# A gated mix of an S4 and an H3 long convolution: the instruction order of three engines listed in the source, and the first gated group's transform moved ahead of the tables

## The chip, the cores and the metric

The kernel runs on one core of a Trainium2 chip, as one launch. The metric is the device time of that core in microseconds. It is given as the median of several executions, beside one execution that the hardware profiler recorded.

## What is computed

A sequence x of 2048 steps and 448 channels in bfloat16 goes through two long causal convolutions, one kernel per channel, and a gate mixes the two:

```python
x = A_u                                                   # [1, 2048, 448]
g = sigmoid((x * gate_w).sum(-1, keepdims=True))
# a: S4. The kernel K is made from 256 complex modes per channel.
logdA = exp(log_dt) * (A_re + 1j * A_im);  dB = exp(log_dt) * (B_re + 1j * B_im)
K = einsum("dn,dnl,dn->dl", C, exp(logdA * l), dB).real   # [448, 2048]
a = causal_conv(x, K) + x * Dskip
# b: H3. A shift convolution of four taps, then a long one with given kernels.
kv = sum(k_shifted_by_t * shift_k[:, t] for t in range(4)) * v
b = x * (causal_conv(kv, ssm_k) + kv * ssm_D)
out = g * a + (1 - g) * b
```

causal_conv is done by FFTs of twice the length in the reference.

## The kernel before

**Groups.** The 448 channels are split into four groups H of 28 channels on each of four partition quarters. Each group goes through the H3 path ("B", H) and the S4 path ("A", H), eight steps in the order B0, B1, B2, A0, B3, A1, A2, A3 (`seq`, L825). Names in code type are tiles as the profile shows them, or functions.

**A convolution as matmuls.** A sequence of one group is `spread` by PE matmuls (L215, PSUM tile `ps_c`), evacuated by ACT to a tile `zs` (`zsK` for an S4 kernel), and `transform`ed in place (L227, matmuls with the constant `s2_W` into `ps`, evacuated by ACT over `zs`). A copy with the two partition halves exchanged, `zsS`, is made by a DMA (L603, function `swapped`). The spectra of two sequences are multiplied on DVE (`products`, L286: first zsS, then zs, times the other's zs). `stage_a` (L265, `ps_a`, evacuated by ACT to `U`) and `stage_b` (L279, `ps_b`, with the constant `sb_G`) go back to the time domain. What ends a group, its epilogue, multiplies ps_b by `uu` into `ug` on DVE (L733, H3) or has ACT copy ps_b to a held tile (S4). The last S4 group is weighted by the gate and added to ug, which is then stored (L743 to L738).

**The S4 kernels.** They are made in eight blocks of 14 channels per quarter, two to a group. First come tables of exponentials: `Tables` builds `ks_hold` (scaled modes, L434), and `chunk(h)` makes one group's table `ET` for two blocks. DVE writes phases to `ks_ph` (L489), ACT takes Sin of them (L493) and Exp of the magnitudes (L481, `ks_mag` and the rows of ET), DVE multiplies (L506). Chunk 0 reads ks_hold in SBUF. `save` (L467) writes ks_hold to DRAM as `xfd`, and later chunks read it back as `ks_xf` (L476). Sin, Exp and Tanh each need an activation table on ACT, and a change between them is a table load. Then `KGen.block(j)` runs: a chain of DVE products and sums (L318 into `kg_P`, L323 into `kg_TQ` and `kg_TP`, L328, L332, L343), 224 matmuls of 21 rows into the one PSUM tile `pk` (L371), an ACT evacuation to `kg_S`, a gather by matmuls (L412, `ps_g` to `kg_KT`), and a spread with the constant WcK (`ps_c` to zsK).

**The front.** SP issues the input DMAs in program order: kt (the H3 k with its halo), the modes, `skraw(0)`, vt, uu, and then, where the source asks for them, `skraw(H)` of the later groups (`load_sk`, L587). `sk_cols` lets GpSimd (POOL) add ssm_D to the first column of skraw (L592), and the spread of KB[H] reads skraw after it. The shift convolution is a DVE product `kvt` (L651), PE sums into `ps_v` (L655) and ACT evacuations to kt; then `kv` = vt times kt (L680, four instructions). XB[H] is the spread and transform of kv. The gate multiplies uu by `gw` into ug (L812, seven instructions), sums by 14 matmuls into `ps_gate` (L815), reduces to `gt` (L817), and takes Tanh; gb and og are its copies. ug has the buffer of vt. `stage_b` of the constants makes `sb_G`: DVE phases `sb_ph`, ACT Sin `sb_v`, DVE multiplies `sb_G`.

**Buffers.** Eight buffers of tag q serve zs, zsS, zsK, kv, U, kvt, modes and the phases. One buffer of tag hq serves skraw, so that skraw(1) is loaded after skraw(0) is read. PSUM has three two-bank tiles of tag ps for everything else, and one for pk and ps_g.

**What sets the order.** The kernel is written as one long program; the framework's scheduler places each engine's instructions by a simulated timeline, with `high_priority` sections ahead of others. Some orders are fixed by hand. `after` ties an instruction behind another on one engine: the DVE chain of a block (`put`), block 0 behind kv, a chunk's phases behind the middle of the block (`kg.mid`), Exp and Sin by turns, s2_W's Sin behind the copy of the taps, and the final `mix` (L769) behind the last block's chain. `behind_other` holds the zsS DMAs of a step (through SP) until `kg_S` of its block is evacuated.

In the source the order around the change is: KB[0]'s spread, transform and swap; kv; chunk 0 and `save`; small constants; skraw(1)'s load and add; XB[0]'s spread, transform and products; the gate; then seven calls of `step(c, n, j)`. A step spreads the next group n, does stage_a of the current group c, transforms n, does stage_b of c, runs block j, and multiplies n's spectra. After them come block 7 and the last S4 group, in halves.

Of the kernel before, what the change touches and what calls it, by code (L numbers as in the profile page):

```python
# [17 lines left out]
P = 128  # L18
# [21 lines left out]


# [15 lines left out]

def low16(ap):
    return ap.bitcast(i16).rearrange("p (n t) -> p n t", t=2)[:, :, 0]


class Consts:

    def __init__(self, tc, pool, scratch):
        self.tc, self.nc, self.pool = tc, tc.nc, pool
        nc = self.nc
        self.scratch, self.used = scratch, 0
        self.pidx = pool.tile([P, 1], i32, name="c_pidx")
        nc.gpsimd.iota(self.pidx[:], pattern=[[0, 1]], base=0, channel_multiplier=1)
# [44 lines left out]
    def stage_2(self, b_col, off_col, big, behind):  # L114
        nc = self.nc
        W = self.pool.tile([P, 32, 2, 64], bf16, name="s2_W")
        j = self.iota("s2_j", [[32, 16], [1024, 64]], base=8)
        for k0 in (0, 16):
            if k0:
                for r in range(2):  # L120
                    nc.vector.scalar_tensor_tensor(out=off_col[r][:], in0=b_col[:], scalar=32.0 * k0, in1=off_col[r][:], op0=ALU.mult, op1=ALU.add)
            ph = big.tile([P, 16, 2, 64], i32, name="s2_ph", tag="kg_TQ", bufs=2)
            for r in range(2):
                self.phases(ph[:, :, r, :], j.rearrange("p (k s) -> p k s", k=16), b_col, off_col[r][:, 0:1])
            sn = nc.scalar.activation(W[:, k0:k0 + 16].rearrange("p k r s -> p k (r s)"),
                                 low16(ph[:].rearrange("p k r s -> p (k r s)")).rearrange("p (k c) -> p k c", k=16), ACT.Sin, scale=PHASE)
            after(self.tc, sn, behind)
        return W
# [11 lines left out]
    def stage_b(self, pool, qt, hqt, k_col, mask):  # L140
        nc = self.nc
        G = pool.tile([P, 64, 2, 4, 32], bf16, name="sb_G")
        jv = self.iota("sb_j", [[8, 16], [512, 32]]).rearrange("p (b a) -> p b a", b=16)
        offs = self.pool.tile([P, 4, 2], f32, name="sb_offs")
        for b0 in range(0, 64, 16):
            ph = qt([P, 16, 2, 32], "sb_ph", i32)
            for r, turn in enumerate((QUARTER, HALF)):
                o = offs[:, b0 // 16, r:r + 1]
                nc.vector.tensor_scalar(out=o, in0=k_col[:], scalar1=8.0 * b0, scalar2=turn, op0=ALU.mult, op1=ALU.add)
                self.phases(ph[:, :, r, :], jv, k_col, o)  # L150
            v = pool.tile([P, 16, 2, 32], bf16, name="sb_v", tag="kg_P4", bufs=2)
            nc.scalar.activation(v[:].rearrange("p b r a -> p (b r a)"), low16(ph[:].rearrange("p b r a -> p (b r a)")),
                                 ACT.Sin, scale=PHASE)
            for g in range(4):
                nc.vector.tensor_scalar(out=G[:, b0:b0 + 16, :, g, :], in0=v[:], scalar1=mask[:, g:g + 1], scalar2=None, op0=ALU.mult)
        return G

# [132 lines left out]
class KGen:  # L290

    def __init__(self, tc, pool, pk, psk, cons, sel_d, d4, ET):
        self.tc, self.nc, self.pk, self.psk = tc, tc.nc, pk, psk
        self.pool, self.cons, self.sel_d, self.d4, self.ET = pool, cons, sel_d, d4, ET

    def block(self, j, evac, behind=None):
# [5 lines left out]

        chain = [behind]

        def put(op):
            if chain[0] is not None:
                after(self.tc, op, chain[0])
            chain[0] = op

        def mult(srcs, e):  # L310
            P4 = self.pool.tile([P, 4, 2, 2, M], bf16, name="kg_P4", tag="kg_P4", bufs=2)
            r = EQ[:, entry_of(e) + 1] if e in Q_LEVELS else EP[:, entry_of(e) - EQ_N + 1]
            i = 0
            for src in srcs:
                m = src.shape[1]
                in0 = src.rearrange("p n c m -> p n (c m)").unsqueeze(2).to_broadcast([P, m, 2, 2 * M])
                in1 = bass.AP(r.tensor, r.offset, [list(r.ap[0]), [0, m], [-M, 2], [1, 2 * M]])
                put(V.tensor_tensor(out=P4[:, i:i + m].rearrange("p n v c m -> p n v (c m)"), in0=in0, in1=in1, op=ALU.mult))  # L318
                i += m
            return P4[:, 0:i].rearrange("p n v c m -> p (n v) c m")  # L320

        def add(T, dst, v):
            put(V.tensor_tensor(out=T[:, dst:dst + v.shape[1] // 2].rearrange("p n v m -> p (n v) m"), in0=v[:, :, 0], in1=v[:, :, 1], op=ALU.add))  # L323

        def back(i0, i1):
            lo = TP[:, 0:16]
            src = bass.AP(lo.tensor, lo.offset + (15 - i0) * 2 * M, [list(lo.ap[0]), [-2 * M, i1 - i0], [M, 2], [1, M]])
            put(V.tensor_tensor(out=TP[:, 16 + i0:16 + i1], in0=src,  # L328
                                in1=EP[:, E_R - EQ_N + i0:E_R - EQ_N + i1].unsqueeze(2).to_broadcast([P, i1 - i0, 2, M]), op=ALU.mult))

        q4 = mult([EQ[:, 0:2].unsqueeze(1)], 4)
        put(V.tensor_copy(TQ[:, 0], EQ[:, 0:2]))  # L332
# [6 lines left out]
        self.mid = chain[0]  # L339
# [3 lines left out]
        put(V.tensor_copy(TP[:, 0], EP[:, 0:2]))  # L343
# [17 lines left out]
        self.last = chain[0]  # L361
# [56 lines left out]
class Tables:  # L418

    def __init__(self, tc, pool, qt, hqt, psum, raw, ident, dt, xfd, dma):  # L420
        nc, V = tc.nc, tc.nc.vector
        self.tc, self.nc, self.pool, self.psum, self.raw, self.ident, self.qt, self.hqt = tc, nc, pool, psum, raw, ident, qt, hqt
        self.xfd, self.dma = xfd, dma
        self.exp, self.sin = None, None
# [44 lines left out]
    def chunk(self, h, behind=None):  # L469
# [7 lines left out]
        x, f = xf[:, :, 0], xf[:, :, 1]  # L477
        turn = 65536.0 / (2.0 * math.pi)

        def exps(dst, e):  # L480
            ex = nc.scalar.activation(dst, x, ACT.Exp, scale=float(e))  # L481
            if self.sin is not None:
                after(self.tc, ex, self.sin)
            self.exp = ex

        def unit(dst, e, off, first):
            ph = self.pool.tile([P, nb, 2, M], i32, name="ks_ph", tag="ks_ph", bufs=2)
            for c in range(2):
                op = V.tensor_scalar(out=ph[:, :, c], in0=f, scalar1=e * turn, scalar2=off + (QUARTER if c == first else 0.0),  # L489
                                     op0=ALU.mult, op1=ALU.add)  # L490
                if behind is not None:
                    after(self.tc, op, behind)
            sn = nc.scalar.activation(dst.rearrange("p b c m -> p b (c m)"),  # L493
                                      low16(ph[:].rearrange("p b c m -> p (b c m)")).rearrange("p (b x) -> p b x", b=nb), ACT.Sin, scale=PHASE)
            after(self.tc, sn, self.exp)
            self.sin = sn
# [24 lines left out]
        for i in range(NR):  # L521
            exps(ET[:, :, E_R + i], 8 * (2 * i + 1))
# [3 lines left out]
def body(  # L526
# [20 lines left out]
    nc = tc.nc  # L547
# [36 lines left out]
    def load_sk(H):  # L584
        raw = hqt([P, NC, 64], "skraw")
# [26 lines left out]
    cons = Consts(tc, wp, kgp.tile([P, 3584], i32, name="scratch", tag="kg_TP"))  # L612
# [17 lines left out]
    for g in range(4):  # L630
        nc.sync.dma_start(vt[g * 32:(g + 1) * 32], v4[g])  # L631
    uu = natt([P, 64, 112], "uu", "natu")
# [13 lines left out]
    wtc = nc.scalar.copy(wt, wraw.rearrange("p l t -> p t l")[:, ::-1])  # L646
# [15 lines left out]
    W2 = cons.stage_2(cons.field("b2", 0, 63), [cons.field("o2%d" % r, 6, 1, -QUARTER, (1 + r) * QUARTER) for r in range(2)], kgp, wtc)  # L662
    k_col, mask_b = cons.field("kB", 2, 31, 4.0, 1.0, pool=wp), cons.onehot("mgB", 4, cons.field("gB", 0, 3), 1.0 / 2048, pool=wp)
    R = cons.stage_a(cons.field("sA", 0, 63), [cons.field("oA%d" % r, 6, 1, HALF, (1 - r) * QUARTER) for r in range(2)])
    tb = Tables(tc, kgp, qt, hqt, psum, raw, ident, dt, xfd, nc.sync)
    tb.coefficients()
    G = cons.stage_b(kgp, qt, hqt, k_col, mask_b)
# [5 lines left out]

    kvq = []
    for H in range(NQG):
# [4 lines left out]
        kvl = V.tensor_tensor(out=kvq[H], in0=q(vt[:]), in1=q(kt[:, 3:67]), op=ALU.mult)  # L680

    ET = kgp.tile([P, 2, ENT, M], bf16, name="ET", tag="kg_E")
    tb.ET = ET
    tb.chunk(0)
    tb.save()

# [19 lines left out]
    kg = KGen(tc, kgp, pk, psk, cons, sel_d, d4, ET)  # L706
# [3 lines left out]
    def block(j):  # L710
        H = j // 2
        if j and j % 2 == 0:
            tb.chunk(H, kg.mid)
        if KA[H] is None:
            KA[H] = qt([P, 32, 4 * NC], "zsK")
        S = kg.block(j, evac, kvl if j == 0 else None)
# [42 lines left out]
    def mix(behind):  # L759
# [7 lines left out]
        for o, a, b, op in ops:  # L767
            for b0 in range(0, 64, 32):
                after(tc, V.tensor_tensor(out=o[:, b0:b0 + 32], in0=a[:, b0:b0 + 32], in1=b[:, b0:b0 + 32], op=op), behind)  # L769

    def kv_cols(H):
        return lambda c: kvq[H][:, :, c]
# [32 lines left out]

    terms, skc = {}, {1: sk_cols(1)}
    XB[0] = spread_in(kv_cols(0))
    transform(nc, psum, W2, XB[0], evac)
    terms["B", 0] = products(nc, *KB[0], XB[0])
# [8 lines left out]
    after(tc, nc.scalar.activation(gt[:], gt[:], ACT.Tanh, scale=0.5), tb.exp)  # L818
# [20 lines left out]
    mix(kg.last)  # L839
# [4 lines left out]
    stage_b(nc, psum, G, U, epilogue_A(3), 1)  # L844

# [34 lines left out]
```

## Time and profile before

| | |
|---|---|
| median of nine executions | 327.13 us (324.03 to 327.67) |
| the profiled execution | 327.57 us, span 325.8 us |
| mean granted TensorE clock in it | 0.816 |
| DVE busy | 273.4 us, 84% of the span, 547 instructions |
| ACT busy | 245.5 us, 75%, 399 instructions |
| PE busy, weight loads | 227.4 us, 70%, and 198.3 us, 61%; 5286 of each |
| POOL busy | 32.1 us, 10%, of which the four adds on skraw 20.9 us |
| DMA | 21.41 MB, mean 66 GB/s |
| chain of waits, by engine | ACT 31%, PE 20%, DVE 20%, SP's queue 14%, DMA 6%, POOL 4%, issue 3% |

The profile gives each engine's busy time, the wait before each instruction and what ended it, and a chain of waits followed back from the last instruction. Times in it are microseconds from the start of the span. A row of a timeline reads: start, duration, engine, line, operation, output tile, input tiles, with partitions and elements of each, and the number of instructions run together. A wait stands in brackets behind. No engine is full over the whole span, so what counts is which one is full in which stretch.

### The profile page before, as it was taken

The numbers are of one execution on the slowest core, as the hardware profiler recorded it, in microseconds if no ns is written. First come the engines' busy times: TensorE is split into PE (matmuls) and PEld (weight loads), VectorE is DVE, ScalarE is ACT, GpSimd is POOL, SyncE is SP. The second block draws the span as 40 slices with busy tenths as digits, with TensorE's granted clock in tenths as the row PEclk, the third lists the DMA queues.
The fourth block names the chain that finished last, engine by engine and source line by source line (L and its number), as shares of the span: only waits on it lengthen the run. The fifth ranks groups of instructions, "written<-read, shape, count | busy, mean of one in ns | idle before, by whom it ended". The sixth has DMA issues, their size and how long they took to land.

```text
span 325.8 us, 11928 instructions
## 1 busy us (share of the span) xinstructions
PE 227.4 (70%) x5286; PEld 198.3 (61%) x5286; DVE 273.4 (84%) x547; ACT 245.5 (75%) x399; POOL 32.1 (10%) x129
## 2 busy tenths in 40 slices
PE   0397507578268677689986797887878989896740
PEld 0144406147258567589986676776768878785640
DVE  7998999925899999999999989699999979617540
ACT  3645879649991799998999999489999658387510
POOL 9400003910000027000000000000000000000000
PEclk9999957658559558767999797998878799797785
DMA  6899999503000530060050014100050005013048
GB/s 133 132 192 160 163 161 179 211 2 57 2 0 4 117 56 3 4 157 3 4 114 6 2 46 92 28 3 2 2 116 3 2 4 117 4 34 84 3 82 145
DMA packets 53740, 21.41 MB, mean 66 GB/s; under 512 B 49080, under 2 KB 52024, under 8 KB 53688
## 3 DMA queue, kind: packets, MB, share of 16 engines
q1 hardware_dynamic: 48936, 19.47, 32.1%
q10 hardware_dynamic: 4560, 1.15, 2.0%
q8 instruction: 41, 0.67, 0.9%
q14 instruction: 11, 0.09, 0.1%
q0 software_dynamic: 192, 0.03, 0.1%
HBM read 10.09 MB, written 3.21 MB: 41 GB/s over the span
## 4 chain that ended last, share of the span: by engine, by line
ACT 31%; PE 20%; DVE 20%; SPq 14%; DMA 6%; POOL 4%; issue 3%; DVEq 0%; POOLq 0%; ACTq 0%
ACT zs L565 10%; DVE kg_P L318 6%; ACT zsK L565 5%; ACT ET L481 5%; PE pk L371 4%; PE ps_a L265 4%; ACT U L565 4%; PE ps_c L215 4%; DMA zsS<-zs 4%; POOL skraw L592 4%; SPq L634 4%; PE ps_b L279 3%; SPq L587 3%; ACT ET L493 2%; SPq L631 2%
## 5 line engine op out<-in xcount | busy, mean ns | idle before, releaser
L565 ACT CAST zs<-ps_c 128x1024 bf16<-128x1024 f32 (+1 forms) x48 | 42.3, 929 | 11.2 <-PE ps_c L215 11.2
L227 PEld LDWEIGHTS <-s_W 128*128 128x128 bf16 x480 | 32.0, 113 | 20.5 <-issue 18.4
L318 DVE TENSOR_TENSOR kg_P<-kg_TQ,ET 128x896 bf16<-128x896 bf16 (+1 forms) x64 | 43.9, 707 | 0.4
L565 ACT CAST zs<-ps 128x896 bf16<-128x896 f32 x48 | 41.3, 923 | 2.1 <-PE ps L227 2.0
L227 PE MATMUL ps<-zs,s_W 128*128 128x112 bf16 x384 | 29.8, 239 | 15.3 <-ACT zs L565 7.8
L265 PE MATMUL ps_a<-sa_R,zs 128*128 128x128 bf16 x196 | 32.7, 258 | 7.7 <-ACT U L565 5.0
L371 PE MATMUL pk<-kg_TP,kg_TQ 128*21 128x32 bf16 x1792 | 31.3, 238 | 5.4 <-issue 3.6
L565 ACT CAST U<-ps_a 128x1024 bf16<-128x1024 f32 (+2 forms) x32 | 28.8, 928 | 5.8 <-PE ps_a L265 3.5
L371 PEld LDWEIGHTS <-kg_TQ 128*21 128x21 bf16 x1792 | 28.2, 121 | 7.5 <-issue 6.3
L265 PEld LDWEIGHTS <-zsS 128*128 128x128 bf16 x196 | 27.9, 156 | 7.9 <-issue 7.9
L279 PE MATMUL ps_b<-U,sb_G 128*128 128x28 bf16 x1024 | 29.1, 176 | 4.9 <-ACT zs L565 1.9
L265 PE MATMUL ps_a<-sa_R,zsS 128*128 128x128 bf16 x196 | 32.4, 257 | 0.0
L279 PEld LDWEIGHTS <-sb_G 128*128 128x128 bf16 x1024 | 27.9, 97 | 6.7 <-issue 5.9
L318 DVE TENSOR_TENSOR kg_P<-kg_TP,ET 128x1792 bf16<-128x1792 bf16 (+1 forms) x32 | 30.9, 966 | 0.0
L592 POOL TENSOR_TENSOR skraw<-skraw,dB 128x28 bf16<-128x28 bf16 x4 | 20.9, 5215 | 95.5 <-DMA skraw<-in_B_ssm_k_dram 95.5
L565 ACT CAST zsK<-ps_c 128x512 bf16<-128x512 f32 (+2 forms) x28 | 22.1, 794 | 8.7 <-PE ps_c L215 8.7
L265 PEld LDWEIGHTS <-zs 128*128 128x128 bf16 x196 | 27.9, 156 | 1.2
L323 DVE TENSOR_TENSOR kg_TQ<-kg_P 128x896 bf16<-128x896 bf16 (+2 forms) x64 | 27.7, 444 | 0.2
L655 PE MATMUL ps_v<-kvt,scratch 128*128 128x448 bf16 x64 | 14.8, 394 | 14.9 <-DVE kvt L651 14.0
L215 PE MATMUL ps_c<-WcK,kg_KT 128*64 128x128 bf16 x224 | 19.5, 303 | 6.6 <-ACT zsK L565 3.4
L493 ACT ACTIVATE ET<-ks_ph 128x448 bf16<-128x448 int16 x40 | 23.0, 589 | 1.1 <-DVE ks_ph L489 0.9
L215 PE MATMUL ps_c<-Wc,kv 128*64 128x128 bf16 x224 | 15.2, 322 | 10.9 <-DVE kv L680 8.6
(142 smaller groups left out, 479.3 us busy)
## 6 DMA issues: line engine op xcount, KB each, us to landing
zsS<-zs SPq DMA_DIRECT2D x16, 448.0 KB, 5.6
kt<-in_B_k_dram SPq DMA_DIRECT2D x16, 112.0 KB, 4.5
skraw<-in_B_ssm_k_dram SPq DMA_DIRECT2D x16, 112.0 KB, 3.8
vt<-in_B_v_dram SPq DMA_DIRECT2D x4, 448.0 KB, 7.0
uu<-in_A_u_dram SPq DMA_DIRECT2D x4, 448.0 KB, 9.0
xfd<-ks_hold SPq DMA_DIRECT2D x2, 672.0 KB, 6.6
ks_xf<-xfd SPq DMA_DIRECT2D x3, 336.0 KB, 3.0
out_dram<-ug SPq DMA_DIRECT2D x8, 112.0 KB, 4.3
```

Source lines behind the costliest of these rows:

```text
L215: nc.tensor.matmul(pt[64 * r:64 * r + 64, i, :], lhsT=x, rhs=W[:, 128 * r:128 * r + 128], start=True, stop=True, tile_position=(0, 64 * r))
L227: nc.tensor.matmul(pt[:, i // 4, (i % 4) * n:(i % 4 + 1) * n], lhsT=W[:, k].rearrange("p r s -> p (r s)"), rhs=zs[:, k], start=True, stop= ...
L265: nc.tensor.matmul(pt[:, i, :], lhsT=t[:].rearrange("p k (g c) -> p (k g) c", g=4)[:, :, j + i], rhs=R[:, 128 * n:128 * n + 128], start=(n ...
L279: nc.tensor.matmul(o, lhsT=G[:, b, r].rearrange("p g a -> p (g a)"), rhs=U[:, r, b], start=(r == 0), stop=(r == 1))
L318: put(V.tensor_tensor(out=P4[:, i:i + m].rearrange("p n v c m -> p n v (c m)"), in0=in0, in1=in1, op=ALU.mult))
L323: put(V.tensor_tensor(out=T[:, dst:dst + v.shape[1] // 2].rearrange("p n v m -> p (n v) m"), in0=v[:, :, 0], in1=v[:, :, 1], op=ALU.add))
L371: nc.tensor.matmul(pt[32 * g:32 * g + NQ, hw, :].rearrange("p (i j) -> p i j", i=2), lhsT=TQ[:, :, c, m], rhs=rhs, start=(hf == 0 and c == 0),
L481: ex = nc.scalar.activation(dst, x, ACT.Exp, scale=float(e))
L493: sn = nc.scalar.activation(dst.rearrange("p b c m -> p b (c m)"), low16(ph[:].rearrange("p b c m -> p (b c m)")).rearrange("p (b x) -> p ...
L565: return nc.scalar.copy(dst, src)
L592: nc.gpsimd.tensor_tensor(out=raw[:, :, 0], in0=raw[:, :, 0], in1=dB[:, H * NC:(H + 1) * NC], op=ALU.add)
L655: nc.tensor.matmul(pt[:, i, 0:448], lhsT=ident, rhs=t[:, n, 4 * i:4 * i + 4, :].rearrange("p b l -> p (b l)"), start=(n == 0), stop=(n == 3))
```

## The change

The change does three things.

First, it adds a table `ORDER` with one permutation each for DVE (547 instructions), ACT (401) and PE (5286). The number of an instruction is its place in the source. A wrapper logs every instruction by engine as the program is built, and at the end `apply` ties each instruction of these three engines behind the one listed before it. These ties are an order on one engine and no waits between engines; each instruction still waits for its data. POOL and SP (with the DMAs that it issues) have no list. With this, all orders by `after` in the old source go; `behind_other` stays.

Second, it moves some source. `chunk` is split into `levels` (phases, Sin, level magnitudes and products) and `reals` (sixteen rows of Exp). XB[0]'s spread, transform and products come right behind kv, ahead of the tables. `stage_b` of the constants stands between `levels(0)` and `reals(0)`, with `save` behind. The phases of chunk 0 take rooms of q buffers, four in each (`ks_ph4`), instead of two small buffers in turn.

Third, the input of group 1's H3 kernel, skraw(1), is loaded ahead of uu into a q buffer of its own, not into the hq buffer.

What the lists do to the order, beside what the diff shows: on DVE, kv, sixteen ks_ph and then four of the gate's ug multiplies follow one another; on PE the 224 pk matmuls of every block stand in a row, and the 14 gate matmuls stand ahead of KB[1]'s spread; on ACT there are 16 table loads where there were 11.

```diff
+ORDER = {
+    "DVE": (
+        "144 17 9 18 11 19-20 29-30 95 97 103 132 119 128-129 105 121 34 10 21 36-37 14-15 12-13 22 111 35 38-39 134 "
...
+    "Activation": (
+        "1 0 2 4 3 15 5-6 16-18 7-14 19-25 27 26 28 37 29 43-44 42 30 39 38 41 32 40 45-47 51 53 49-50 54 56 52 58 48 "
...
+    "PE": (
+        "0-509 662-885 510-661 971-1002 886-902 1003-1018 903-958 1019-1058 959-964 1059-1146 1331-1554 965-970 "
...
+class Order:
+
+    def __init__(self, tc):
+        self.tc, self.log = tc, {}
+        for e in ("vector", "scalar", "tensor", "gpsimd", "sync"):
+            setattr(self, e, Listed(self.log, getattr(tc.nc, e)))
+
+    def apply(self):
+        for engine, text in ORDER.items():
+            seq = []
+            for run in text.split():
+                a, _, b = run.partition("-")
+                seq.extend(range(int(a), int(b or a) + 1))
+            log = self.log[engine]
+            assert sorted(seq) == list(range(len(log)))
+            for a, b in zip(seq, seq[1:]):
+                after(self.tc, log[b], log[a])
...
-                put(V.tensor_tensor(out=P4[:, i:i + m].rearrange("p n v c m -> p n v (c m)"), in0=in0, in1=in1, op=ALU.mult))
+                V.tensor_tensor(out=P4[:, i:i + m].rearrange("p n v c m -> p n v (c m)"), in0=in0, in1=in1, op=ALU.mult)
...
-    def chunk(self, h, behind=None):
+    def chunk(self, h):
+        self.levels(h)
+        self.reals(h)
+
+    def reals(self, h):
+        for i in range(NR):
+            self.exps(self.ET[:, :, E_R + i], 8 * (2 * i + 1))
...
         def unit(dst, e, off, first):
-            ph = self.pool.tile([P, nb, 2, M], i32, name="ks_ph", tag="ks_ph", bufs=2)
+            if h:
+                ph = self.pool.tile([P, nb, 2, M], i32, name="ks_ph", tag="ks_ph", bufs=2)
+            else:
+                if not room:
+                    four = self.qt([P, 4, nb, 2, M], "ks_ph4", i32)
+                    room.extend(four[:, i] for i in range(4))
+                ph = room.pop(0)
...
-        raw = hqt([P, NC, 64], "skraw")
+        raw = (qt if H == 1 else hqt)([P, NC, 64], "skraw")
...
+    sk1 = load_sk(1)
     uu = natt([P, 64, 112], "uu", "natu")
...
     tb.coefficients()
-    G = cons.stage_b(kgp, qt, hqt, k_col, mask_b)
...
-        kvl = V.tensor_tensor(out=kvq[H], in0=q(vt[:]), in1=q(kt[:, 3:67]), op=ALU.mult)
-
+        V.tensor_tensor(out=kvq[H], in0=q(vt[:]), in1=q(kt[:, 3:67]), op=ALU.mult)
+    def kv_cols(H):
+        return lambda c: kvq[H][:, :, c]
+    XB[0] = spread_in(kv_cols(0))
+    transform(nc, psum, W2, XB[0], evac)
+    term0 = products(nc, *KB[0], XB[0])
     ET = kgp.tile([P, 2, ENT, M], bf16, name="ET", tag="kg_E")
     tb.ET = ET
-    tb.chunk(0)
+    tb.levels(0)
+    G = cons.stage_b(kgp, qt, hqt, k_col, mask_b)
+    tb.reals(0)
     tb.save()
...
-            tb.chunk(H, kg.mid)
+            tb.chunk(H)
...
-    terms, skc = {}, {1: sk_cols(1)}
-    XB[0] = spread_in(kv_cols(0))
-    transform(nc, psum, W2, XB[0], evac)
-    terms["B", 0] = products(nc, *KB[0], XB[0])
+    terms, skc = {("B", 0): term0}, {1: sk_cols(1, sk1)}
...
+    nc.apply()
```

## The prediction

> **What bounds the kernel now.** I read the stages first: busy time of each engine from one milestone to the next. The columns are the stretch and its length, then busy us of PE, weight loads, DVE, ACT and POOL, the granted clock, DMA share and GB/s.
>
> ```profile
> 54.50:66.50 12.00, 5.97 (x38) 2.91 (x35) 11.82 (x26) 7.15 (x10) 12.00 (x1) 0.69 0.60 191
> 66.50:81.50 15.00, 12.53 (x164) 10.44 (x165) 5.34 (x19) 11.62 (x18) 0.34 (x2) 0.68 0.20 32
> 107.00:202.00 95.00, 75.28 (x1869) 68.72 (x1869) 91.84 (x192) 90.95 (x163) 7.89 (x1) 0.79 0.22 48
> 202.00:272.70 70.70, 59.16 (x1646) 54.28 (x1645) 65.49 (x129) 57.06 (x93) 0.00 (x0) 0.88 0.15 35
> 272.70:325.80 53.10, 33.20 (x857) 31.08 (x857) 24.77 (x29) 26.09 (x34) 0.00 (x0) 0.80 0.30 58
> ```
>
> From 81.5 to 272.7 us DVE is all but full: this is the chain of the eight kernel blocks. Between 66.5 and 81.5 it works 5.34 of 15.00 us. The chain of waits says why:
>
> ```profile
> 50.54 3.78 DMA skraw<-in_B_ssm_k_dram
> 54.48 12.04 POOL skraw L592
> 66.56 0.85 PE ps_c L215 x12
> ```
>
> The one POOL add on skraw holds PE and, behind it, ACT. DVE's and ACT's timelines show the waits that follow from it, the start of block 0, and three later waits of DVE:
>
> ```profile
> 69.63 1.93 ACT L565 CAST zs<-ps_c 128x1024 bf16<-128x1024 f32 x2 [7.35 <-PE ps_c L215]
> 69.27 0.69 DVE L817 TENSOR_REDUCE gt<-ps_gate 128x64 f32<-128x512 f32 x1 [2.95 <-PE ps_gate L815]
> 73.80 0.39 DVE L506 TENSOR_TENSOR ET<-ET,ks_mag 128x448 bf16<-128x448 bf16 x1 [3.84 <-ACT ET L493]
> 81.54 0.39 DVE L318 TENSOR_TENSOR kg_P<-ET 128x448 bf16<-128x448 bf16 x1
> 107.03 0.53 ACT L565 CAST kg_S<-pk 128x448 bf16<-128x448 f32 x1 [7.82 <-PE pk L371]
> 206.53 2.03 DVE L286 TENSOR_TENSOR zsS<-zsS,zs 128x3584 bf16<-128x3584 bf16 x1 [3.03 <-DMA zsS<-zs]
> 262.57 0.22 DVE L343 COPY kg_TP<-ET 128x224 bf16<-128x224 bf16 x1 [1.91 <-PE pk L371]
> ```
>
> Brackets give the idle time before and what ended it. Last, SP's own queue, whose order the change alters:
>
> ```profile
> 33.26 12.06 SPq L634 DMA_DIRECT2D uu<-in_A_u_dram  x4
> 45.42 6.42 SPq L587 DMA_DIRECT2D skraw<-in_B_ssm_k_dram  x4
> ```
>
> **What the Trainium skill says.** "SBUF — State Buffer", section "Who interferes with whom": a DVE instruction with two SBUF inputs and a GpSimd instruction that reads SBUF exclude each other. The trace agrees: the skraw add takes 0.61 us at 28.49 and 0.34 at 77.42, both inside DVE gaps, but 12.03 us at 54.48, ending 0.2 us after DVE runs dry at 66.3. "ScalarE: Activation LUTs", section "What ACT_TABLE_LOAD costs": 1283 ns a load, and a drain of 1.38 us. The trace has the 1283 ns and no drain: the load at 46.96 is followed by an exp at 48.25. I use 1.283. "DMA: Bandwidth & Descriptors", section "Issuing engines are not separate DMA queues": all transfers share 16 engines. The stage 28.5 to 54.5 has these at full share with 161 GB/s, so what is issued earlier delays what comes after.
>
> **The change, part by part.** The sum is made against the profiled execution, 327.57 us (span 325.8 and 1.8 around it; the median of nine is 327.13). Positions are those of the two built orders.
>
> *Inputs.* The four loads of skraw(1), 112 KB each, now stand ahead of uu's four, in a q buffer of its own. They land near 42, and the POOL add has a DVE gap near 49 to run in. The 12.04 us leave the chain. But uu is now last: in before it landed by about 42.42 + 9.0 = 51.4 and skraw(1) at 54.3; with the places exchanged uu lands at 54.3 to 56, I take 55. skraw(2)'s loads also move ahead of the xfd and zsS transfers: 0.45 MB at 161 GB/s is 2.8 us on those; zsS then lands near 64, before its reader at 68.
>
> *DVE up to block 0.* The kvt stage starts and runs as now, with 1.1 us more small work in it, so the first ks_hold is at 31.2 instead of 30.1. Eight sb_ph (3.7) and eight sb_G (3.3) leave the stretch before kv; kv runs 42.2 to 46.3 (47.85 to 51.86 now), sixteen ks_ph (0.19 apart) to 49.3. The next listed are four ug multiplies, which need uu: **DVE stands from 49.3 to 55**, new idle of 5.7. Then, in listed order: ug x4 2.5 (57.5), ET x4 1.2, ug and ET 0.9 (59.6), six ks_ph and table steps with two sb_ph to 62.9, ET, two ug and four sb_ph to 66.7, four sb_G 1.6 (68.3), the products zsS and zs 3.9 (72.2), the gate reduce 0.7 (72.9), two sb_ph 0.9, eight sb_G 3.2, WcK and small ones to 78.05. There block 0 starts: 81.54 - 78.05 = 3.5 earlier, though 1.6 of sb_G is still owed. Block 0 itself is 16.8 us of own work in before; with 1.6 sb_G, 0.6 ks_ph, 0.5 gate steps and 0.6 of block 1 ahead it ends at 98.1, against 101.5: **-3.4**.
>
> *ACT up to the first kg_S.* The list holds 16 table loads against 11: five more, 6.4 us. XB[0]'s third evacuation stands behind the ET sins, one of which waits for a DVE product behind uu: it comes at 61.6, the transform is out at 67.1, in time for 68.3. From 67.1: loads, exps, sb_v and evacuations of KB[1] and XB[1] one after another give 91.6 before U, 95 after it, three zs evacuations 97.5, load and five table steps 102.7. PE's first pk block starts at 98.1, and takes 4.9 with its issue gap as now: kg_S at 103 against 107.03. The five loads are covered by the 7.35 and 7.82 of ACT idle; without these they would cost 6.4.
>
> *Blocks 1 to 4.* DVE idles 3.2 of the 95 us, ACT 4.1. Both are full, so at most 3.2 comes back; the 1.28 before kg_TP at 192.3 should go, since PE's list puts pk ahead of other work. I take **-1.6** (0 to -3.2).
>
> *Block 5.* The B(3) product that waits 3.03 stands in the new list after five more steps of the block (about 7 us): **-3.0**.
>
> *Blocks 6, 7 and the end.* A(1)'s products come 2.3 us of DVE work later, but PE takes block 6's pk first (DVE is done with it at 254.5 - 3.9 = 250.6 of before, where PE now starts ps_a at 253.8). The wait of 1.91 at 262.57 goes and pk of block 7 can start at 270.8 instead of 275.04. The two ug,og multiplies now precede A(2)'s products, which end 0.8 later, at 279.2; ps_a follows there instead of 281.3: **-2.0**. After that the order is the same but for ps_b and ps_c, which no longer alternate: 0.
>
> *New waits.* A list that is followed to the letter has waits that I can't see one by one. Bounds: 0, and the 5.2 us that DVE idles now in 202 to 272.7. I take +2.4. Other edits (Sin text, helper arguments, high_priority) only feed the order: 0, nothing hides behind them.
>
> Sum: -3.4 - 1.6 - 3.0 - 2.0 + 2.4 = **-7.6**, 320.0 us.
>
> **Rivals.** *uu comes as early as now* (51.4): 3.6 more at the front, and no new waits: 327.6 - 3.4 - 3.6 - 3.2 - 3.0 - 2.0 = 312.4. For it: the 16 engines may serve both loads side by side. Against: 161 GB/s is what this stage gets at full share.
>
> *The step chain, not the block chain, sets the end.* KB[1]'s spread moves behind the gate sums, to 71 to 73 from 66.6, and U from 84.4 to 91.6. If products of step 1 follow that and not kg_S, the front gain is lost and 3 us more: about 326.4, no difference. Against: the zsS transfer of step 1 is issued at 107.59, right after kg_S at 107.03.
>
> *Slower: PE's whole pk blocks.* Before, pk of two blocks is cut in pieces (26, 18, 45, 135 and 22, 62, 57, 83 matmuls) between ps_a, ps_c and ps_b, where PE would wait for evacuations. The list runs each as 224 in a row, in front of transforms, so those waits stay open and 3.9 us comes on top, twice: 7.8. In 107 to 202 PE idles 19.7 and hides it; in 202 to 272.7 it idles 11.5. It decides once the open waits pass that 11.5; then the front and the tail gain nothing and the time is 327.6 + 7.8 - 3.0 - 1.6 = 330.8. A list that doesn't take effect is excluded: the built orders differ.
>
> **How the numbers follow.** Forecast 0.57, the early uu 0.13, both faster: 0.70. The step chain 0.08, no difference. PE's blocks or another listed wait of that size 0.22, slower. What a measurement of this kernel can tell from no change is about 0.5% (1.6 us). The forecast's own range is 316 (no new waits, all of 3.2 back) to 325 (5.2 of new waits and nothing from blocks 1 to 4). To leave out no more than 2 in 10 the range runs from 313 to 329.
>
> **What would show it.** Right: a DVE wait on uu of 4 to 7 us near 50; the skraw(1) add under 1 us or inside that wait; block 0 starting near 78; the first kg_S near 103; no 3 us wait on zsS; ps_a of the last A step near 271. Wrong: block 0 after 81.5, kg_S later than 107, or DVE waits of over 8 us in blocks 1 to 5.

## The result, and the profile after

The changed kernel takes 325.94 us (median of 16 executions, 324.77 to 326.96) against 327.13 us before. The ratio is 0.9971, with a 95% interval of 0.9952 to 0.9991. The forecast was 320.0 us; of its 7.6 us about one is there. The profiled execution of the changed kernel took 326.96 us, the longest of its 16, with a span of 325.1 us. All its lines are L113, that of the wrapper, so rows are told apart by their tiles.

The stages, with the columns of the prediction (stretch, length, busy us of PE, weight loads, DVE, ACT and POOL, clock, DMA share, GB/s):

```profile
54.50:66.50 12.00, 4.19 (x37) 3.53 (x37) 11.84 (x32) 7.73 (x13) 0.42 (x1) 0.53 0.83 239
66.50:81.50 15.00, 6.18 (x83) 4.19 (x81) 14.41 (x29) 14.61 (x21) 0.00 (x0) 0.70 0.01 2
107.00:202.00 95.00, 76.89 (x1992) 70.90 (x1991) 93.77 (x183) 86.09 (x155) 1.26 (x1) 0.81 0.20 44
202.00:272.70 70.70, 59.10 (x1718) 54.82 (x1720) 66.56 (x125) 59.84 (x99) 0.00 (x0) 0.93 0.18 42
272.70:325.10 52.40, 33.08 (x836) 31.27 (x824) 23.77 (x27) 24.67 (x31) 0.00 (x0) 0.74 0.29 55
```

From 66.5 to 81.5 us DVE now works 14.41 us where it worked 5.34. The hole before block 0 is closed. In the two long stretches of the blocks DVE is busy 1.93 and 1.07 us more than before, with fewer instructions in them (183 against 192, and 125 against 129).

DVE's timeline shows the wait for uu, the start of block 0, the largest wait in the blocks, and the products of B(3), which no longer wait:

```profile
54.59 2.50 DVE L113 TENSOR_TENSOR ug<-uu,gw 128x1024 bf16<-128x1024 bf16 x4 [4.54 <-DMA uu<-in_A_u_dram]
77.92 0.39 DVE L113 TENSOR_TENSOR kg_P<-ET 128x448 bf16<-128x448 bf16 x1
209.72 0.22 DVE L113 COPY kg_TP<-ET 128x224 bf16<-128x224 bf16 x1 [2.25 <-PE pk L113]
213.45 2.03 DVE L113 TENSOR_TENSOR zsS<-zsS,zs 128x3584 bf16<-128x3584 bf16 x1
```

In the chain of waits the transfer of uu now stands where skraw(1) and the POOL add stood:

```profile
45.16 9.31 DMA uu<-in_A_u_dram
54.59 2.50 DVE ug L113 x4
```

ACT's timeline shows why the first kg_S, forecast for 103, comes at 105.68 although the pk matmuls end at 103.57. In the list two Sins stand ahead of it, and each waits for phases from DVE:

```profile
103.27 0.58 ACT L113 ACTIVATE ET<-ks_ph 128x448 bf16<-128x448 int16 x1 [1.54 <-DVE ks_ph L113]
103.75 0.56 ACT L113 ACTIVATE ET<-ET 128x448 bf16<-128x448 bf16 x1
105.20 0.58 ACT L113 ACTIVATE ET<-ks_ph 128x448 bf16<-128x448 int16 x1 [0.89 <-DVE ks_ph L113]
105.68 0.52 ACT L113 CAST kg_S<-pk 128x448 bf16<-128x448 f32 x1
```

### A cost that no row shows

Four rows of DVE's timeline of the kernel before, from block 7, and four of the changed kernel, from block 1, tell where DVE's added time lies. Read start plus duration against the next start.

```profile
262.89 0.62 DVE L318 TENSOR_TENSOR kg_P<-kg_TQ,ET 128x896 bf16<-128x896 bf16 x1
263.43 0.62 DVE L318 TENSOR_TENSOR kg_P<-kg_TP,ET 128x896 bf16<-128x896 bf16 x1
263.97 0.38 DVE L323 TENSOR_TENSOR kg_TQ<-kg_P 128x448 bf16<-128x448 bf16 x1
264.27 0.39 DVE L323 TENSOR_TENSOR kg_TP<-kg_P 128x448 bf16<-128x448 bf16 x1
```

```profile
113.61 0.61 DVE L113 TENSOR_TENSOR kg_P<-kg_TQ,ET 128x896 bf16<-128x896 bf16 x1
114.26 0.39 DVE L113 TENSOR_TENSOR kg_TQ<-kg_P 128x448 bf16<-128x448 bf16 x1
114.56 1.08 DVE L113 TENSOR_TENSOR kg_P<-kg_TP,ET 128x1792 bf16<-128x1792 bf16 x1
115.68 0.63 DVE L113 TENSOR_TENSOR kg_TP<-kg_P 128x896 bf16<-128x896 bf16 x1
```

Before, two products and then two sums alternate, and each instruction starts 0.08 us before the end of the one ahead, as far as the records tell (262.89 + 0.62 = 263.51, the next at 263.43). In the list a sum stands right behind its own product. It starts 0.04 us after its end (113.61 + 0.61 = 114.22, the next at 114.26). Over all DVE records from block 0 to 285 us the means are 0.082 before the end and 0.034 after it: a neighbour that reads the result just made costs 0.116 us more. I call this a stall. There are 23 such neighbours before and 83 in the changed kernel, so by this count 60 x 0.116 = 7.0 us are lost. No bracket shows them, since the gaps are too short to be waits.

The table splits DVE's time from block 0's first step to the end of A(2)'s products into three parts, added up from the DVE records of each profiled execution. Work is the durations less what neighbours overlap, plus the short gaps; waits are gaps over 0.12 us. "Dependent" counts the short gaps after an unfinished result. The kernels below the first two are those of the experiments.

| kernel | start | end | work | dependent | waits |
|---|---|---|---|---|---|
| before | 81.54 | 278.44 | 187.4 | 23 | 9.5 |
| changed | 77.92 | 280.76 | 199.7 | 83 | 3.1 |
| results and readers apart | 78.09 | 280.12 | 192.5 | 19 | 9.6 |
| apart, third ks_ph room | 77.50 | 278.08 | 192.3 | 18 | 8.3 |
| uu first | 75.59 | 277.68 | 199.6 | 83 | 2.5 |
| uu first, apart | 74.75 | 276.57 | 192.6 | 21 | 9.2 |
| uu first, apart, third room | 74.19 | 273.03 | 192.2 | 18 | 6.7 |
| changed, fifteen negations less on ACT | 77.94 | 280.17 | 199.3 | 82 | 2.9 |
| apart, fifteen negations less on ACT | 77.55 | 276.12 | 192.3 | 20 | 6.3 |

From before to changed the work grows by 12.3 us. Two og multiplies (2.02 us each) now stand inside the stretch and no longer behind it, 4.0. The lost overlap is 27.86 - 23.48 = 4.4 and the short gaps grow from 0.79 to 2.84, 2.1; these make 6.4 for the dependent neighbours of this stretch. Most of the remaining 1.8 is four sb_G multiplies (0.48 each) that block 0 took over, less three small steps that now come ahead of it. The waits fall by 6.4, the same number as the stalls.

### The profile page after: what moved, and what is told of

Its sections match the earlier page's. It is cut to its first block, busy times and chain, and to the rows that moved or that the text cites. A ratio compares the mean times of both kernels' runs of the same rounds, so it can differ in the third digit from the quotient of the medians.

```text
span 325.1 us, 11932 instructions
## 1 busy us (share of the span) xinstructions
PE 221.4 (68%) x5286; PEld 196.2 (60%) x5286; DVE 281.2 (87%) x547; ACT 251.7 (77%) x404; POOL 21.1 (6%) x129
## 4 chain that ended last, share of the span: by engine, by line
DVE 34%; ACT 24%; PE 17%; SPq 12%; issue 5%; DMA 4%; DVEq 0%; ACTq 0%
SPq L113 12%; DVE kg_P L113 11%; ACT zs L113 7%; DVE kg_TP L113 6%; PE ps_c L113 5%; ACT ET L113 5%; ACT U L113 4%; DVE kg_TQ L113 4%; ACT zsK L113 4%; PE ps_b L113 3%; PE pk L113 3%; PE ps L113 3%; DVE ug L113 3%; DMA uu<-in_A_u_dram 3%; PE ps_a L113 2%
## 5 line engine op out<-in xcount | busy, mean ns | idle before, releaser
L113 PEld LDWEIGHTS <-s_W 128*128 128x128 bf16 x544 | 33.6, 110 | 32.8 <-issue 31.0
L113 ACT CAST zs<-ps_c 128x1024 bf16<-128x1024 f32 (+1 forms) x48 | 42.3, 918 | 4.1 <-PE ps_c L113 3.8
L113 DVE TENSOR_TENSOR kg_P<-kg_TQ,ET 128x896 bf16<-128x896 bf16 (+1 forms) x64 | 44.5, 707 | 0.5
L113 PE MATMUL ps<-zs,s_W 128*128 128x112 bf16 x384 | 29.1, 236 | 23.0 <-ACT zs L113 19.6
L113 ACT CAST zs<-ps 128x896 bf16<-128x896 f32 x48 | 41.6, 925 | 0.7 <-PE ps L113 0.7
L113 PE MATMUL ps_a<-sa_R,zs 128*128 128x128 bf16 x224 | 37.3, 260 | 3.4 <-DVE zs L113 1.3
L113 PE MATMUL pk<-kg_TP,kg_TQ 128*21 128x32 bf16 x1792 | 29.8, 238 | 12.9 <-issue 9.2
L113 PE MATMUL ps_a<-sa_R,zsS 128*128 128x128 bf16 x224 | 36.8, 258 | 0.0
L113 PEld LDWEIGHTS <-kg_TQ 128*21 128x21 bf16 x1792 | 27.7, 121 | 14.9 <-issue 12.2
L113 ACT CAST U<-ps_a 128x1024 bf16<-128x1024 f32 (+2 forms) x32 | 28.8, 940 | 6.4 <-PE ps_a L113 6.4
L113 PEld LDWEIGHTS <-zsS 128*128 128x128 bf16 x224 | 32.1, 156 | 2.3 <-issue 2.3
L113 PEld LDWEIGHTS <-zs 128*128 128x128 bf16 x224 | 32.0, 156 | 2.4 <-DVE zs L113 1.6
L113 PE MATMUL ps_b<-U,sb_G 128*128 128x28 bf16 x1024 | 28.0, 176 | 5.4 <-ACT zs L113 2.6
L113 PEld LDWEIGHTS <-sb_G 128*128 128x128 bf16 x1024 | 27.4, 97 | 6.4 <-issue 5.6
L113 DVE TENSOR_TENSOR kg_P<-kg_TP,ET 128x1792 bf16<-128x1792 bf16 (+1 forms) x32 | 30.9, 968 | 0.1
L113 DVE TENSOR_TENSOR kg_TQ<-kg_P 128x896 bf16<-128x896 bf16 (+2 forms) x64 | 28.1, 447 | 1.0
L113 PE MATMUL ps_v<-kvt,scratch 128*128 128x448 bf16 x64 | 14.7, 386 | 16.8 <-DVE kvt L113 16.8
L113 ACT ACTIVATE ET<-ks_ph 128x448 bf16<-128x448 int16 x40 | 22.4, 590 | 3.5 <-DVE ks_ph L113 2.4
L113 ACT CAST zsK<-ps_c 128x512 bf16<-128x512 f32 (+2 forms) x28 | 21.6, 779 | 3.7 <-PE ps_c L113 3.6
L113 PE MATMUL ps_c<-Wc,kv 128*64 128x128 bf16 x224 | 16.2, 320 | 9.8 <-ACT zs L113 7.6
L113 PEld LDWEIGHTS <-kv 128*64 128x64 bf16 x224 | 15.3, 220 | 10.9 <-issue 8.4
```

Of the source, the lines that this page charges most:

```text
L113: ins = f(*args, **kw)
```

## The experiments

Theory: the front gain is real, and the dependent neighbours in DVE's list took back most of it. Rivals: ACT, full in 160 to 190, sets the pace; PE's whole pk blocks do; or the front's own waits ate the gain. Ratios are to the kernel before.

**Results and readers apart.** The same lists, but DVE's rearranged; a piece of it:

```diff
...
-        "236-237 235 201 200 238-240 202-203 206 242-243 241 204 207 205 208-210 245-246 156 244 248-249 247 157 "
-        "251-252 211-212 214 213 215 221 254-255 253 189-190 216 218 217 220 250 257 219 222-223 258-265 256 266-270 "
...
+        "202-203 206 242-243 241 204-205 207-210 245-246 156 244 248-249 247 157 251-252 211-215 254 221 255 253 189 216 "
+        "190 218 217 220 250 257 219 222 258 223 259-265 256 266-270 274 272 271 275 273 295 276-288 294 290 296 191 297 "
...
```

> The changed kernel with one edit: the DVE list is rearranged locally so that a DVE instruction seldom stands right behind the one whose result it reads. 125 of the 547 places change, each by at most 4 places; the ACT and PE lists and all else are the same. In the profiled executions, from the first step of block 0 to 285 us, DVE starts an instruction 0.082 us before the end of the one ahead where that one is independent, and 0.034 us after its end where it reads its result; there are 23 such dependent neighbours in the kernel before and 83 in the changed one, and 10 should be left here. Theory (the 60 more dependent neighbours, 0.116 us each, ate 7.0 us of the gain): DVE's work shrinks by 73 x 0.116 = 8.5 us, of which the path takes most; time 317 to 321, ratio to before 0.970 to 0.981. Rival (PE and ACT, by their lists, set the pace of the blocks; DVE then only waits more): 324.5 to 327, ratio 0.993 to 1.0, with the DVE waits on pk and on ACT grown by about 7 us in 100 to 280.

Measured: 324.18 us, ratio 0.9921 (0.9896 to 0.9946), 0.5% under the changed kernel. The time lies next to the rival's range and far from the theory's: the stalls were not simply time that the kernel lost. Each named half of it: DVE's work shrank by 7.2 us, near the 8.5 of the theory (19 dependent neighbours are left, not 10), and its waits grew by 6.4, as the rival says. The profiled execution was the longest of this kernel (325.93 us), so the table's end time is a late one. DVE's timeline of this kernel shows where the waits are:

```profile
158.19 0.46 DVE L112 TENSOR_SCALAR ks_ph<-ks_xf 128x224 int32<-128x224 f32 x2 [0.91 <-ACT ET L112]
201.36 0.28 DVE L112 TENSOR_SCALAR ks_ph<-ks_xf 128x224 int32<-128x224 f32 x1 [1.10 <-ACT ET L112]
208.33 0.22 DVE L112 COPY kg_TP<-ET 128x224 bf16<-128x224 bf16 x1 [2.02 <-PE pk L112]
221.37 0.28 DVE L112 TENSOR_SCALAR ks_ph<-ks_xf 128x224 int32<-128x224 f32 x1 [2.26 <-ACT ET L112]
```

A write of ks_ph that waits for a Sin on ACT waits for a room: there are two, and the Sin is their reader. With others like these, 5.5 of the 9.6 us stand in front of ks_ph, and 3.0 for pk. The rearranging has a part in this itself: four of these writes, with 4.3 of the 5.5 us, stand one to four places further ahead in the new list. The last of the rows above now stands ahead of three steps of the block that DVE could have run meanwhile. So this run does not measure the stalls quite alone; the third room below takes most of these waits away.

**Sums behind their products, in the kernel before.** This tries the disputed cost without lists.

```diff
-        q256 = mult([TQ[:, 0:4]], 256)
-        q1 = mult([TQ[:, 0:4]], 1)
-        add(TQ, 8, q256)
-        add(TQ, 4, q1)
+        add(TQ, 8, mult([TQ[:, 0:4]], 256))
+        add(TQ, 4, mult([TQ[:, 0:4]], 1))
...
```

> The kernel before with one edit: in the DVE chain of a block each sum stands right behind the product that it reads, where before two products and then two sums alternated. The instructions are the same, no list, no other move. Sums right behind their own product go from 6 to 67 in the built order, 61 more. Theory: 61 x 0.116 = 7.1 us more on DVE; the 7.7 us in which it waits in 100 to 275 takes up some of it, so 331 to 334, ratio 1.012 to 1.021. Rival (DVE's stalls are hidden, as ACT and PE bound the blocks): 326 to 328.5, ratio 0.997 to 1.004.

Measured: 331.62 us, ratio 1.0141 (1.0100 to 1.0182), 4.8 us more. The time lies in the theory's range: from block 0 to 285 us the profile counts 79 dependent neighbours where there were 23 (81 up to 290 us), and the instructions are the same. But their order is not held here, and the scheduler also put A(2)'s products ahead of part of block 7's chain:

```profile
275.90 2.03 DVE L286 TENSOR_TENSOR zsS<-zsS,zsK 128x3584 bf16<-128x3584 bf16 x1 [0.48 <-ACT zsK L554]
287.60 2.09 DVE L328 TENSOR_TENSOR kg_TP<-kg_TP,ET 128x1792 bf16<-128x1792 bf16 x2
```

That chain ends at 289.7 instead of 272.7, and up to the end of the products DVE's waits are 13.7 us, not 9.5. So the 4.8 us are not shown to be the stalls alone; how they split stays open.

**skraw(1) early, in the kernel before.**

```diff
-        raw = hqt([P, NC, 64], "skraw")
+        raw = (qt if H == 1 else hqt)([P, NC, 64], "skraw")
...
+    sk1 = load_sk(1)
     uu = natt([P, 64, 112], "uu", "natu")
...
-    terms, skc = {}, {1: sk_cols(1)}
+    terms, skc = {}, {1: sk_cols(1, sk1)}
```

> The kernel before with one part of the change: skraw(1) is loaded ahead of uu into a q buffer. No lists, no moved transform. Theory (the POOL add held up KB[1]'s spread and with it ACT and the tables): the add takes under 2 us instead of 12, block 0 starts 3 to 4 us before 81.5, and 2 to 4 us of it reach the end: 323 to 325, ratio 0.988 to 0.994. Rival (uu, which lands some 4 us later, takes its place on DVE, and the spectra products wait for a later zsS): block 0 starts at 80 to 82, time 326 to 328, ratio 0.997 to 1.003.

Measured: 325.22 us, ratio 0.9944 (0.9918 to 0.9970), just above the theory's range. This part alone brings no less than the whole change does (0.9971; the intervals overlap). The add takes 1.27 us instead of 12.03, as the theory says, but block 0 starts at 80.24, as the rival says: 1.3 us earlier. In front of it DVE waits five times for a Sin on ACT, 6.8 us in all; in the kernel before four such waits have 6.9. So the add was the last of several waits; the rest of the 3.6 us that the whole change brings to block 0 is left to the moved transform and the lists, which no run takes apart.

**uu first, in the changed kernel.** `sk1 = load_sk(1)` is moved behind the loads of uu, and stays in its q buffer.

> The changed kernel with one part undone: skraw(1) is loaded behind uu again, still into its own q buffer. Theory (DVE stands at the head of its list for uu, which costs the front 4.5 us): uu lands 3 to 4 us earlier, the DVE wait near 50 shrinks from 4.5 to about 1, block 0 starts near 75, and the time is 322 to 324.5 if nothing else is late. Rival (the POOL add, now without a DVE gap, ends only near 70 and KB[1]'s spread comes late again, or the tables on ACT set block 0's start): block 0 at 77 to 80, time 325 to 328.

Measured: 323.10 us, ratio 0.9864 (0.9816 to 0.9912). The time and block 0's start, at 75.59, are as the theory says. The wait on uu in DVE's timeline is now

```profile
51.80 2.50 DVE L113 TENSOR_TENSOR ug<-uu,gw 128x1024 bf16<-128x1024 bf16 x4 [1.76 <-DMA uu<-in_A_u_dram]
```

The POOL add takes 2.68 us at 54.77, although DVE leaves no gap there. The exchange of the two loads, taken alone, costs the changed kernel some 3 us (2.8 by the medians, 3.5 by the ratios).

**Both edits.**

> The changed kernel with both edits: the DVE list with results and readers apart, and uu loaded ahead of skraw(1). Theory (two separate costs: the stand for uu in the front, and the stalls in the blocks): the ratios multiply, 0.9864 x 0.9921 / 0.9971 = 0.9815, 320 to 322. Rival (what DVE saves in the blocks is lost to ACT, and an earlier front too): no better than with uu first alone, 322.5 to 324, ratio 0.985 to 0.991.

Measured: 321.36 us, ratio 0.9847 (0.9814 to 0.9879). The time lies in the theory's range, the ratio at the edge of the rival's, and beside uu first alone (0.9864) the intervals overlap. So the run does not tell the two apart.

**Less work on ACT, with and without DVE's stalls.** The list is the same with the fifteen places taken out.

```diff
-                nc.scalar.mul(B[:, :, :, 2], B[:, :, :, 0], -1.0)
+                if h == 0:
+                    nc.scalar.mul(B[:, :, :, 2], B[:, :, :, 0], -1.0)
```

> The changed kernel without the fifteen ACT negations that make the third row of each level of ET for the chunks 1 to 3 (the rows of chunk 0 are used in their place), and with the ACT list without these; 8.5 us of ACT work between 103 and 233 us are left out. Theory (DVE with its stalls sets the pace of the blocks, ACT only stands beside it): 0 to 1.5 us less than the changed kernel, 324.4 to 326, ratio 0.992 to 0.998. Rival (ACT sets the pace, being full in 160 to 190 and 210 to 237): 3 to 6 us less, 320 to 323, ratio 0.979 to 0.988.

> The changed kernel with DVE's results and readers apart, and without the same fifteen ACT negations of the chunks 1 to 3. Theory (once DVE no longer stalls, ACT is next: DVE waited 5.5 us on ET there): 2.5 to 5 us less than with the list alone, 319 to 322, ratio 0.976 to 0.985. Rival (PE, with its undivided pk blocks, is next): within 1 us of it, 323 to 325, ratio 0.989 to 0.995.

Measured: 325.67 us, ratio 0.9960 (0.9941 to 0.9979), for the changed kernel: 8.5 us of ACT work are worth nothing that can be told. That refutes ACT as what paces the changed kernel. With results and readers apart it is 322.71 us, ratio 0.9888 (0.9852 to 0.9924), between the two expectations; the interval overlaps that of the kernel with the work left in (0.9896 to 0.9946), so whether ACT is next there stays open.

**A third room for ks_ph.**

```diff
-                ph = self.pool.tile([P, nb, 2, M], i32, name="ks_ph", tag="ks_ph", bufs=2)
+                ph = self.pool.tile([P, nb, 2, M], i32, name="ks_ph", tag="ks_ph", bufs=3)
...
-            t = kgp.tile([P, 32, NC], bf16, name="ept")[:, 0:n]
+            t = kgp.tile([P, 32, NC], bf16, name="ept", tag="ks_ph", bufs=3)[:, 0:n]
```

> The changed kernel with DVE's results and readers apart, and a third room for the phases ks_ph of the chunks 1 to 3 (it shares the rooms with the tile ept of the last epilogue, which needs none before 305 us). With the rearranged list alone DVE waited 5.5 us in front of ks_ph writes until a Sin on ACT had ended. Theory (that is a wait for one of the two rooms, and it is what took the place of the stalls): these waits fall under 2 us and the time is 2 to 4.5 us under that of the rearranged list alone, 319.5 to 322.5, ratio 0.977 to 0.986. Rival (Sin itself is late on ACT, so DVE waits as long at the next product of ET or for pk): within 1 us of it, 323 to 325.5, ratio 0.989 to 0.9955.

> The changed kernel with the third room for ks_ph and nothing else. Theory (there DVE stalls set the pace and it waits 0.9 us in all for ET): 0 to 1 us less than the changed kernel, 325 to 326.3, ratio 0.9945 to 0.998. Rival (the rooms held the changed kernel too, through ACT): 2 us less or more, ratio under 0.992.

> The changed kernel with three edits: results and readers apart, uu ahead of skraw(1), a third room for ks_ph. Theory as for the third room alone: 2 to 4.5 us under the two edits without it (ratio 0.9847), 317 to 320, ratio 0.970 to 0.979. Rival: within 1 us of it, 320.5 to 322.5, ratio 0.981 to 0.988.

Measured: on the changed kernel 326.05 us, ratio 0.9963 (0.9944 to 0.9983), nothing, as the theory says. With results and readers apart 322.77 us, ratio 0.9880 (0.9840 to 0.9919): 0.4% less than without the room, under what the theory asked, and the intervals overlap. With uu first as well **318.37 us, ratio 0.9757 (0.9712 to 0.9802)**, within the theory's range, 0.9% under the two edits without the room (the intervals do not overlap) and the fastest kernel here. In the second, the waits in front of ks_ph fall from 5.5 us to the first row below, but others come up at the next product of ET, and pk stays; together they are still 8.3 us:

```profile
200.79 0.28 DVE L112 TENSOR_SCALAR ks_ph<-ks_xf 128x224 int32<-128x224 f32 x1 [1.20 <-ACT ET L112]
207.57 0.22 DVE L112 COPY kg_TP<-ET 128x224 bf16<-128x224 bf16 x1 [2.32 <-PE pk L112]
220.70 0.39 DVE L112 TENSOR_TENSOR ET<-ET,ks_mag 128x448 bf16<-128x448 bf16 x1 [0.99 <-ACT ET L112]
```

These runs also give a cleaner price of the stalls. With the third room in both kernels, setting results and readers apart brings 0.8% (0.9880 against 0.9963, intervals apart), some 2.7 us.

**Without the PE list, and without any.** The first leaves out the entry "PE" of ORDER, the second the call of `apply`.

> The changed kernel without the PE list: the scheduler places PE's instructions, DVE and ACT keep theirs. In the built order three of the eight pk blocks are then cut (86 and 138, 172 and 52, 220 and 4 matmuls) where the list runs 224 in a row. Theory (PE's whole pk blocks are not what ate the gain; DVE waits only 2.3 us for pk in the changed kernel): no gain from it, 325 to 329, ratio 0.994 to 1.006. Rival (the whole pk blocks, which the prediction priced at 7.8 us, hold the blocks): 4 us or more less than the changed kernel, 318 to 322, ratio 0.972 to 0.985.

> The changed source without the lists: the scheduler orders all engines, and the old ties by hand are gone too. The built order has 23 table loads (16 with the lists, 11 before) and 6 sums right behind their product (51 and 6). Theory (the lists carry what is gained; seven more loads, 9 us, and the lost ties cost): 330 to 342, ratio 1.01 to 1.045. Rival (the moved source and the earlier skraw(1) carry it, the lists add nothing): 321 to 326, ratio 0.98 to 0.997.

Measured: 335.14 us, ratio 1.0227 (1.0194 to 1.0260), and 349.83 us, ratio 1.0683 (1.0625 to 1.0742). Neither size was foreseen. The direction of the first speaks against the rival of PE's whole blocks, though it changes all of PE's order and cuts only three of the eight blocks: with PE's order left to the scheduler DVE waits 12.1 us in the stretch of the table, not 3.1. Two of these waits are

```profile
217.78 2.02 DVE L103 TENSOR_TENSOR zsS<-zsS,zs 128x3584 bf16<-128x3584 bf16 x1 [2.72 <-ACT zs L103]
286.63 2.03 DVE L103 TENSOR_TENSOR zsS<-zsS,zsK 128x3584 bf16<-128x3584 bf16 x1 [3.62 <-ACT zsK L103]
```

## Why the prediction was wrong, point by point

- **Inputs and DVE's front: right.** uu ended DVE's wait at 54.59 (55 taken), the wait was 4.54 us (5.7), and block 0 started at 77.92 (78.05). Block 0's last step ended at 98.98 (98.1); the missing 0.9 is its first share of dependent neighbours, 14 in the block where there were 4. The skraw(1) add left the chain, but neither in under 1 us nor inside the wait on uu: it took 7.16 us from 43.06. It cost nothing there, as the spread that reads skraw came only at 68.65. The reading that the short adds of the kernel before lie inside DVE gaps is wrong: at 28.49 DVE worked on to 28.91, and the one at 77.42, 0.34 long, ran into an instruction that DVE started at 77.51.
- **ACT's front: 2.7 us off.** The five added table loads all fall before 81 us, as worked out. kg_S was put behind the table steps, at 103, without the two Sins' waits for DVE, 1.54 and 0.89.
- **The waits in the blocks (-1.6 and -3.0, new ones +2.4): near as a sum, wrong as a saving.** No wait of DVE is left from 78 to 205 us, the 3.03 before the B(3) products is gone, and the new ones in 205 to 223 sum to 3.1. But this came with a slower DVE. Where DVE is not slower (results and readers apart, with nearly the same lists) there are 9.6 us of waits, as many as in the kernel before, and 8.3 with a third room. Stalls had taken the place of most of the waits.
- **The step that failed** is the price of the blocks: "Block 0 itself is 16.8 us of own work in before", and every other block likewise. Durations were taken over unchanged although the list changes neighbours, so the cost of dependent neighbours stood at nothing, without a reason. It measured +6.4 in the stretch (7.0 up to 285 us), which is the size of the miss: 320.0 + 6.4 = 326.4, measured 325.94. With that price the kernel's time would have come out, but not what the stalls are worth: the forecast left some 4 us of DVE waits in the stretch (an estimate from its own terms: 9.5 in the kernel before, less 1.1 in block 0, 1.6, 3.0 and 1.9, with 2.4 new), and without the stalls there are 8.3 to 9.6.
- **The tail (-2.0): right as a mechanism, on too late a start.** The last A step's ps_a now follows A(2)'s products at once, as forecast: 0.05 us behind them, where it stood 2.83 behind. But these products end at 280.76. On the clock of before I had put that end at 279.2, and the earlier gains were to come off it; they did not arrive. So ps_a, which was to start near 271, starts at 280.81 against 281.27. What the two og multiplies ahead of the products cost, 4.0 us of work, no run measures alone.
- **Its sums.** The terms named for the upper end of the range, 325, give 324.4. The sign for ps_a, 271, leaves out the 2.4 of new waits; with them it is 273.7. Neither bears on the outcome.
- **The rivals.** The early uu was right in kind: uu first gives some 3 us (3.6 priced), but the 312.4 built on it left out the same term. The step chain came near the measured time, 326.4, but not for its reason: the zsS transfer of step 1 is issued at 106.22, right after kg_S, as the text against it said. PE's whole blocks would have given 330.8; the time is far below it, the blocks have one wait of DVE for pk, 2.25 us, and without the PE list the kernel is slower.

That the stalls lengthen DVE's work is shown by the table: 7.2 us less without them. The kernel before with sums behind products (+4.8 us) fits this, but its order changed too. That taking them away gives the changed kernel 1.6 us (0.9971 - 0.9921, 0.5%), or some 2.7 where a third room is there in both, and not 7 is shown too. The table says where the rest goes: into waits, for ks_ph rooms and pk first of all. Stalls and rooms lie side by side, so that neither edit alone brings much: apart from the front, the room alone 0.1% (within the noise), the stalls alone 0.5%, both together 0.9% (0.9971 to 0.9880), and with uu first 1.1% (0.9864 to 0.9757). What holds the last 6.7 us of waits, ACT's place for Sin or PE's for pk, stays open.

## What to carry to other kernels

A list of instructions is priced by its neighbours, not only by its rows: count how often an instruction reads what the one right ahead of it on DVE wrote, and put independent work between. When waits vanish from a profile, look whether the engine was sped up or only slowed to the pace of what it waited for; a removed stall pays only as far as the next buffer. An exchange of two loads is a trade: price the one that becomes last by who stands at the head of a list for it.

## What was not expected of the hardware

On DVE an instruction that does not read the last result starts 0.082 us before its predecessor's end in the records, and one that does 0.034 us after it, for every form in the chain from 128x224 to 128x1792. The wait on a semaphore is not what costs: in the changed kernel, from block 0 to 285 us, 86 independent instructions carry a wait on DVE's own semaphore too, and they start 0.083 us before their predecessor's end all the same. The Trainium skill's page "VectorE: DVE Perf Modes", section "The DRAIN you can't avoid", has it that the next operation waits for an empty pipe, that one that is not held starts earlier, and that a semaphore behind each of eight copies costs nothing extra. The traces agree on the semaphore; the 0.116 us between an independent and a dependent neighbour are what they add.

The POOL add on skraw(1) took 7.16 us in the changed kernel, and ended at 50.22, just after DVE had come to stand for uu at 50.05:

```profile
43.06 7.16 POOL L113 TENSOR_TENSOR skraw<-skraw,dB 128x28 bf16<-128x28 bf16 x1 [13.12 <-DMA skraw<-in_B_ssm_k_dram]
```

With the third room, in a kernel whose front is the same, it took 0.64 us at 42.61, beside DVE instructions without a gap. So it is not a gap on DVE alone that makes this add short, and what decides between 0.6 and 7 us stays open.
